# FNet and mixture-of-experts kernel: half of six blocks' residuals by an adding DMA, a check moved among the experts, two rows' statistics on VectorE

## Chip, core and metric

One core of a Trainium2 chip. The metric is the device time of one execution in microseconds (us). The engines that matter are TensorE (PE, matmuls; PEld is its weight load), VectorE (DVE), ScalarE (ACT), GpSimd (POOL), and SyncE (SP), which issues most DMAs. Each engine runs its own queue in order and waits at semaphores for the others.

## What is computed

Two layers on 2048 tokens of width 512, cut to the core:

```python
x = A_x
# FNet: Fourier transform over hidden and sequence, real part
n = layernorm(x)
a = einsum("bsd,ed->bse", n, dft_hid_re)
b = einsum("bsd,ed->bse", n, dft_hid_im)
h = x + einsum("ts,bse->bte", dft_seq_re, a) - einsum("ts,bse->bte", dft_seq_im, b)
# mixture of 8 experts, each token to its best one (gate: softmax of one value)
f = layernorm(h)
e = argmax(f @ w_gate)
h2 = h + gate * (silu(f @ w1[e]) @ w2[e])
```

## The kernel before

**First stage (0 to some 235 us): the FNet.** The sequence-side transform comes first. The 2048 rows of `x` arrive in four groups ("quads") `xq[0..3]` of 512 rows, that is four row tiles q of 128 rows each. For each group VectorE and ScalarE compute the layer norm's statistics (`far_stats` on ScalarE for the row tiles in `SIDE`, `own_stats` on VectorE for the others), fold the rows (`turned`, `mirror`, `mix`) and round them into `xh[g]` (`spread`) and into `fold[g]` (`high` for the high part `fh`, `low_part` for the low part `fl`).

The matrix of the sequence transform arrives in 32 blocks n, each for a 256-column chunk c and a group g (`PLAN`): blocks 0 to 7 are chunks 0 and 1 of groups 0 to 3 in turn, two blocks per group, while the later blocks belong to one chunk after another. A block is two loads of 512 KB, `raw` i = 0 and i = 1 (`load_w`, four buffers in a ring). `high_w(n)` has ScalarE copy 256 + 256 + 256 columns of the first half into `hold` (rounded to fp32r, the third part negated). `rest_w(n)` has VectorE form the residual of each half, `raw` minus or plus a window of `hold`, into `pair` (line 367): four row tiles of 512 columns, q = 0, 1 from i = 0 and q = 2, 3 from i = 1. TensorE multiplies: `residual` (line 720) takes `pair` against `xh[g]`, `folded` (line 731) takes `hold` against `fold[g]`, `outer` (line 735) two edge rows. The first four groups are one Python loop over g; blocks 2g and 2g + 1 are used in group g. When chunk 0 is summed (after block 6), `evacuate` copies its sums from PSUM (ScalarE lines 686 to 700, VectorE 692). From block 8 on (`step`) the loop is over chunks; in the first of these steps also the hidden-side matrices `dh`, `ds`, `dd` are prepared (`prep_d`, lines 408 to 422), and `second` (line 644) multiplies the evacuated chunk by them, token tile by token tile, beside the next chunks.

**A check.** The roundings only hold if the residuals are small. `gauge(n)` queues, for every block, ScalarE's sum of squares of the residuals q = 1 to 3 (`square`, line 371), one for each block into `rsum`, and for g = 0 that of `hold` into `hsum`; `settle` puts queued squares into the order a few blocks later. After the FNet, `order()` (in steps among the first expert's) compares them, and `ctl` says whether a slow repair at the end must run.

**Second stage (to some 545 us): the experts.** Eight experts r, 11 steps j each. In a step, `prep` makes the next step's weights: ScalarE rounds a 512 KB load (`far`, in the first expert `raw`) into the high half of `pair` (line 131) and VectorE subtracts the low half (line 132); `first` does 12 matmuls `hp` from them, ScalarE the Silu, VectorE `hh` and `hl`; `then` does the second product two steps later. GpSimd gathers and scatters token rows by indirect DMAs; `o` and `yT` are VectorE's and ScalarE's outgoing tiles.

**What sets the order.** On TensorE, VectorE, ScalarE and SP the order is that of the Python code (`manual_schedule`). GpSimd's is set by the scheduler of the language. A DMA that waits for a semaphore holds up what is queued behind it on its issuing engine.

Of the kernel before, what the change touches and what calls it, by code (L numbers as in the profile page):

```python
# [8 lines left out]
F32 = mybir.dt.float32  # L9
F32R = mybir.dt.float32r  # L10
# [3 lines left out]
ALU = mybir.AluOpType  # L14
# [11 lines left out]
NC = S // TC  # L26
NJ = (F + P - 1) // P

DEFER = 4
HOT = (1, 0, 2, 3)  # L30
EARLY, LATE = 240, 64
# [26 lines left out]
def fnet_moe(ctx: ExitStack, tc: tile.TileContext, xquad, xedge, xres, wseq, wedge, dhid, dmix, wcol, wexp, out):  # L58
# [44 lines left out]
    peek = const.tile([NL, 8], F32, name="peek")  # L103
    nc.vector.tensor_scalar(base, start_at, float(EARLY - P), 1.0, op0=ALU.is_lt, op1=ALU.add)
    rsum = const.tile([P, NT], F32, name="rsum")
    hsum = const.tile([P, NC], F32, name="hsum")
    rsumd = const.tile([P, KD], F32, name="rsumd")
    hsumd = const.tile([P, KD // 2], F32, name="hsumd")
# [84 lines left out]
    with ExitStack() as pa:  # L193
# [7 lines left out]
        def ap(t, at, dims):  # L201
            return bass.AP(tensor=t.tensor, offset=t.offset + at, ap=[list(t.ap[0])] + dims)
# [139 lines left out]
        def load_w(n, some=range(2)):  # L342
            if n < NT:
                c, g = PLAN[n]
                for i in some:
                    t = wraw[n, i] = ring.tile([P, 2 * D], F32, name="raw", bufs=RAWS)
                    nc.sync.dma_start(t, wseq[c, g, i])

        def high_w(n):
            settle(n - 4)  # L350
            if n < NT:
                a = wraw[n, 0]
                h = his[n] = hbuf[:, n % QN, :]
                nc.scalar.copy(h[:, :2 * TC], a[:, :2 * TC])
                nc.scalar.mul(h[:, 2 * TC:], a[:, :TC], -1.0)  # L355

        def rest_w(n, some=range(2)):

            if n >= NT:
                return  # L360
            if n not in res:
                res[n] = ring.tile([P, QN, D], F32R, name="pair", bufs=4)
            window = ap(his[n].bitcast(F32), 0, [[TC, 2], [1, 2 * TC]])
            odd = ORDER[PLAN[n][0]][0]
            for i in some:
                w = wraw.pop((n, i)).rearrange("p (q c) -> p q c", q=2)
                nc.vector.tensor_tensor(res[n][:, 2 * i:2 * i + 2, :], w, window, op=ALU.add if odd and i else ALU.subtract)  # L367

        def square(out, src, n):
            junk = work.tile([P, 3 * D], BF16, name="junk", bufs=1)  # L370
# [3 lines left out]

        def gauge(n):

            c, g = PLAN[n]
            at = c * QN + g
            r, h = res[n][:, 1:, :].rearrange("p q c -> p (q c)"), his[n][:, TC:2 * TC]
            pending.append((n, lambda: square(rsum[:, at:at + 1], r.bitcast(F32), 3 * D)))  # L380
            if g == 0:
                pending.append((n, lambda: square(hsum[:, c:c + 1], h.bitcast(F32), TC)))
# [3 lines left out]
                pending.pop(0)[1]()  # L386
                most -= 1

        dh, ds, dd = [[keep.tile([P, 2, D], F32R, name=f"{n}{i}") for i in range(KD // 2)] for n in ("dh", "ds", "dd")]
        wk = keep.tile([P, KD, E], F32, name="wk")  # L390
        draw = {}

# [368 lines left out]

        def prep_w(n):
            rest_w(n)
            load_w(n + 2)

        xes, first_e = prep_xe(), prep_e(0)

# [32 lines left out]
        spread(0, CB, r2)  # L800
        rest_w(0, (1,))
        load_w(2)

        for g in range(QN):
# [341 lines left out]
    with ExitStack() as pb:  # L1146
# [169 lines left out]
        def order():  # L1316
# [40 lines left out]
            nbs = work.tile([P, 1], F32, name="nbs")  # L1357
            nc.vector.reduce_sum(nbs, nb, axis=AX.X)
            nc.vector.tensor_copy(nbi, nbs)
            yield  # L1360
            good = work.tile([P, NT + KD], F32, name="good")
            most = work.tile([P, NC], F32, name="most")
            nc.vector.tensor_scalar(most, hsum, SMALL, None, op0=ALU.mult)
# [16 lines left out]
            nc.vector.tensor_scalar(ctl[:, 2:3], fine, float(NC), None, op0=ALU.mult)  # L1380
            nc.vector.tensor_add(fine, fine, nbs)
            nc.vector.tensor_scalar(ctl[:, 0:1], fine, 0.0, None, op0=ALU.is_gt)

        def look_up(r):

# [9 lines left out]
        ordering = order()  # L1395

        for n in range(len(steps) + LAG):
            if n < len(steps):
# [2 lines left out]
                    prep(NA + n + 1)  # L1401
                if r == 0 and j:
                    next(ordering, None)
                if r + 1 < E:

                    if j == (3 if r == 0 else 0):
                        look_up(r + 1)
                        wheres[r + 1] = whence(tab[r + 1][0])
                    if j == (4 if r == 0 else 1):
                        xgs[r + 1] = gather("xg", frows, wheres[r + 1][0], pieces(CAPS[r + 1]))  # L1410
                    if j == 8:
                        src, ids = wheres.pop(r + 1)
                        hgs[r + 1] = gather("hg", hrows, src, pieces(CAPS[r + 1])), ids, tab[r + 1][1]
# [10 lines left out]
            if n >= LAG:  # L1424
# [14 lines left out]
                    going = back(hgs.pop(q), yT, pieces(CAPS[q]))  # L1439
                if j < NQ and r:  # L1440
                    next(going, None)
        q, yT = done.pop()
        for _ in back(hgs.pop(q), yT, pieces(CAPS[q])):
            pass
# [279 lines left out]
```

## Time and profile before

| | |
|---|---|
| median of 3 runs | 557.08 us (556.95 to 558.57) |
| the profiled execution | 556.46 us, span of the trace 554.7 us |
| busy, TensorE | 523.7 us, 94% |
| busy, VectorE | 421.0 us, 76% |
| busy, ScalarE | 313.2 us, 56% |
| mean granted TensorE clock | 0.966 |
| HBM read | 99.63 MB |

Shares of the whole span mix two stages with different limits, so a table of busy times by stretch comes first, then who waited for whom in a stretch, then the single instructions of an engine in order of time. A row of the timeline is: start, duration, engine, line and operation, out<-in, form, count, and in brackets the idle time before it and who ended it.

### The profile page before, as it was taken

How to read it: one execution, taken by the hardware profiler on the slowest of the kernel's cores; microseconds unless marked ns; L12 is line 12 of the kernel's file. 1: busy time of each engine (PE TensorE's matmuls, PEld its weight loads, DVE VectorE, ACT ScalarE, POOL GpSimd, SP SyncE). 2: the span in 40 equal slices, each digit the busy share in tenths (PEclk: the TensorE clock that was granted, in tenths of full speed). 3: DMA queues.
4: the chain of work that ended last, by engine and by line, in shares of the span. 5: the costliest groups of instructions: out<-in, count | busy, mean ns of one | idle time of the engine just before them, and what ended most of it. 6: DMA issues, size and time to landing. Idle time of an engine off the chain costs nothing. (4 is left out here: it accounts for less than half of the span.)

```text
span 554.7 us, 9722 instructions
## 1 busy us (share of the span) xinstructions
PE 523.7 (94%) x3478; PEld 477.1 (86%) x3478; DVE 421.0 (76%) x916; ACT 313.2 (56%) x566; POOL 80.2 (14%) x112
## 2 busy tenths in 40 slices
PE   6886979999999999999999999999999999999992
PEld 2665768999998999998999999999999999999991
DVE  6999999997886678767686766867778777777751
ACT  5799985659582555465544444445455555555540
POOL 2000000000000000001250620431503223130201
PEclk9586998999999999999999999999999999999997
DMA  8767647565767666545185664765757667585401
GB/s 309 250 229 254 209 166 259 188 208 193 253 225 238 209 210 223 182 157 195 48 308 229 224 207 146 229 198 194 220 196 228 230 228 264 182 275 186 151 1 43
DMA packets 36458, 112.95 MB, mean 204 GB/s; under 512 B 4670, under 2 KB 4670, under 8 KB 36400
## 3 DMA queue, kind: packets, MB, share of 16 engines
q1 hardware_dynamic: 32144, 99.38, 54.2%
q0 software_dynamic: 4256, 12.85, 6.7%
q8 instruction: 30, 0.49, 0.4%
q14 instruction: 28, 0.23, 0.1%
HBM read 99.63 MB, written 12.78 MB: 203 GB/s over the span
## 5 line engine op out<-in xcount | busy, mean ns | idle before, releaser
L132 DVE TENSOR_TENSOR pair<-far,pair 128x1024 fp32r<-128x1024 f32 x77 | 94.3, 1225 | 55.2 <-ACT pair L131 55.2
L131 ACT CAST pair<-far 128x1024 fp32r<-128x1024 f32 x77 | 80.9, 1050 | 75.7 <-PE yp L167 75.7
L720 PE MATMUL p<-pair,xh 128*128 128x512 f32 (+1 forms) x480 | 104.0, 344 | 16.9 <-DVE pair L367 12.9
L720 PEld LDWEIGHTS p<-pair,xh 128*128 128x128 f32 x480 | 78.2, 203 | 30.0 <-DVE pair L367 12.7
L165 PE MATMUL hp<-th,pair 128*128 128x256 f32 (+3 forms) x308 | 88.3, 287 | 0.0
L166 PE MATMUL hp<-tl,pair 128*128 128x256 f32 (+3 forms) x308 | 87.4, 284 | 0.0
L167 PE MATMUL hp<-th,pair 128*128 128x256 f32 (+3 forms) x308 | 87.3, 283 | 0.0
L367 DVE TENSOR_TENSOR pair<-raw,hold 128x1024 fp32r<-128x1024 f32 x64 | 75.7, 1217 | 7.0 <-ACT hold L355 4.1
L1211 ACT ACTIVATE sl<-hp 128x256 f32<-128x256 f32 (+4 forms) x88 | 34.7, 395 | 48.5 <-PE hp L167 48.5
L731 PE MATMUL p<-hold,fh 128*128 128x256 f32 x240 | 59.6, 288 | 0.0
L165 PEld LDWEIGHTS hp<-th,pair 128*128 128x128 f32 x308 | 58.0, 188 | 1.9
L166 PEld LDWEIGHTS hp<-tl,pair 128*128 128x128 f32 x308 | 57.9, 188 | 1.6
L167 PEld LDWEIGHTS hp<-th,pair 128*128 128x128 f32 x308 | 57.9, 188 | 0.0
L165 PE MATMUL yp<-hh,pair 128*128 128x304 f32 (+3 forms) x176 | 52.8, 300 | 0.0
L166 PE MATMUL yp<-hl,pair 128*128 128x304 f32 (+3 forms) x176 | 51.2, 291 | 0.0
L167 PE MATMUL yp<-hh,pair 128*128 128x304 f32 (+3 forms) x176 | 51.2, 291 | 0.0
L371 ACT ACTIVATE junk<-pair 128x1536 bf16<-128x1536 f32 x32 | 47.3, 1479 | 0.0
L731 PEld LDWEIGHTS p<-hold,fh 128*128 128x128 f32 x240 | 45.1, 198 | 1.1
L731 PE MATMUL p<-hold,fl 128*128 128x256 f32 x152 | 42.8, 291 | 0.0
L1259 POOL DMA_INDIRECT out_h<-o,ids x20 | 30.4, 1520 | 79.9 <-DVE o L1258 79.1
L1215 DVE TENSOR_TENSOR hl<-sl,hh 128x256 fp32r<-128x256 f32 (+4 forms) x88 | 38.5, 438 | 3.0
L165 PE MATMUL yp<-pair,hl 128*128 128x512 f32 x88 | 35.8, 407 | 0.0
(322 smaller groups left out, 1078.5 us busy)
## 6 DMA issues: line engine op xcount, KB each, us to landing
far<-in_wexp SPq DMA_DIRECT2D x77, 512.0 KB, 3.7
raw<-in_wseq SPq DMA_DIRECT2D x64, 512.0 KB, 4.7
raw<-in_wexp SPq DMA_DIRECT2D x11, 512.0 KB, 4.4
big<-in_xquad SPq DMA_DIRECT2D x8, 512.0 KB, 5.8
xt<-in_xres SPq DMA_DIRECT2D x16, 256.0 KB, 5.3
hrows<-row SPq DMA_DIRECT2D x16, 256.0 KB, 4.5
frows<-row SPq DMA_DIRECT2D x13, 256.0 KB, 4.6
big<-in_dmix SPq DMA_DIRECT2D x3, 512.0 KB, 6.6
```

The lines of the kernel that those rows point to most:

```text
L131: nc.scalar.copy(hi, src)
L132: (eng or nc.vector).tensor_sub(lo, src, hi.bitcast(F32))
L165: nc.tensor.matmul(ps, sl, mh, start=first, stop=False)
L166: nc.tensor.matmul(ps, sh, ml, start=False, stop=False)
L167: nc.tensor.matmul(ps, sh, mh, start=False, stop=last)
L367: nc.vector.tensor_tensor(res[n][:, 2 * i:2 * i + 2, :], w, window, op=ALU.add if odd and i else ALU.subtract)
L371: nc.scalar.activation(junk[:, :n], src, AF.Square, accum_out=out)
L720: nc.tensor.matmul(out, xh[g][:, q, k * P:(k + 1) * P], mv, start=first, stop=False)
L731: nc.tensor.matmul(out, s, mv, start=False, stop=False)
L1211: nc.scalar.activation(sl, ps, AF.Silu)
L1215: nc.vector.tensor_sub(hl, sl, hh.bitcast(F32))
L1259: d = nc.gpsimd.indirect_dma_start(out=out, out_offset=bass.IndirectOffsetOnAxis(ap=ids[:n, i:i + 1], axis=0), in_=o[:n], in_offset=None, ...
```

## The change

1. For the six blocks 2 to 7 (`ADDS`), the residual of the second half (q = 2, 3) is no longer formed by VectorE from a loaded `raw`. GpSimd issues a DMA that copies the window of `hold` into the block's place, and behind it a DMA that adds the block's second half from DRAM onto it (`accum_op`). In these blocks `load_w` loads only the first half, which lets loads be issued earlier (`LOADS`). Blocks 2, 3 and 4 get places of their own, `homes`, a tile in which later `dh`, `ds` and `dd` lie.
2. `high_w` of the odd blocks moves: block 3 to the end of the first group's preparation, block 5 and 7 likewise, one group earlier than before.
3. `gauge` does nothing for blocks 0 to 7. In its place `recheck` loads both halves of each of these blocks again (16 loads of 512 KB) among the experts from the second on, in `raw` buffers; ScalarE copies and negates, VectorE forms both residuals (128x512 and 128x1024), ScalarE squares them; one piece in each step, six steps for a block. The comparison and `ctl` follow it.
4. `SIDE[2]` is empty: all four rows' statistics of group 3 are VectorE's.

```diff
+ADDS = range(2, 8)
+LOADS = {1: (4, 5), 2: (6,), 3: (7,), 4: (8,), 5: (), 6: (9,), 7: ()}
+ANEW = 8
...
                 for i in some:
+                    if i and n in ADDS:
+                        continue
                     t = wraw[n, i] = ring.tile([P, 2 * D], F32, name="raw", bufs=RAWS)
                     nc.sync.dma_start(t, wseq[c, g, i])
...
                 h = his[n] = hbuf[:, n % QN, :]
                 nc.scalar.copy(h[:, :2 * TC], a[:, :2 * TC])
                 nc.scalar.mul(h[:, 2 * TC:], a[:, :TC], -1.0)
+                if n in ADDS:
+                    c, g = PLAN[n]
+                    nc.gpsimd.dma_start(home(n)[:, 2:4, :], windows(n))
+                    nc.gpsimd.dma_start(home(n)[:, 2:4, :], wseq[c, g, 1].rearrange("p (q c) -> p q c", q=2), accum_op=ALU.add)
...
             for i in some:
+                if i and n in ADDS:
+                    continue
                 w = wraw.pop((n, i)).rearrange("p (q c) -> p q c", q=2)
...
         def gauge(n):
 
+            if n < ANEW:
+                return
...
-        SIDE = (CB,(3,),CB)
+        SIDE = (CB,(3,),())
...
-            high_w(2 * g + 1)
+            if not g:
+                high_w(1)
...
                 settle(2 * g - 1)
+                high_w(2 * g + 3)
                 upper(g + 1, r2)
...
+        def recheck():
+
+            for n in range(ANEW):
+                c, g = PLAN[n]
+                at = c * QN + g
+                a, b = [ring.tile([P, 2 * D], F32, name="raw", bufs=RAWS) for _ in range(2)]
+                for i, t in enumerate((a, b)):
+                    nc.sync.dma_start(t, wseq[c, g, i])
+                yield
+                yield
+                h = ring.tile([P, 2 * D], F32, name="raw", bufs=RAWS)
+                nc.scalar.copy(h[:, :D].bitcast(F32R), a[:, :D])
+                nc.scalar.mul(h[:, D:D + TC].bitcast(F32R), a[:, :TC], -1.0)
+                yield
+                nc.vector.tensor_sub(a[:, D:], a[:, D:], h[:, TC:TC + D])
+                yield
+                window = bass.AP(tensor=h.tensor, offset=h.offset, ap=[list(h.ap[0]), [TC, 2], [1, D]])
+                b2 = b.rearrange("p (q c) -> p q c", q=2)
+                nc.vector.tensor_tensor(b2, b2, window, op=ALU.add if ORDER[c][0] else ALU.subtract)
+                nc.scalar.activation(a[:, D:], a[:, D:], AF.Square, accum_out=rsum[:, at:at + 1])
+                yield
+                if g == 0:
+                    nc.scalar.activation(h[:, TC:2 * TC], h[:, TC:2 * TC], AF.Square, accum_out=hsum[:, c:c + 1])
+                nc.scalar.activation(b, b, AF.Square, accum_out=rsum1[:, at:at + 1])
+                yield
...
+                if r > 0:
+                    next(checking, None)
```

GpSimd's queue, from its last small constants to the first DMA of the second half of the FNet. Before, nothing stands there:

```order
L125 MEMSET xlow_105 2x1 x3
L125 MEMSET wlow_106 4x1 x3
L1009 DMA peek_99<-frows_144 13x8
L1012 MEMSET hold_2825 128x1
L1085 TENSOR_SCALAR src0_2911<-table_96 128x2
```

With the change (L370 is the copy of a `hold` window, L371 the adding DMA; `homes_169` holds blocks 2, 3 and 4, `pair_481` block 5, `pair_590` block 6, `pair_631` block 7):

```order
L129 MEMSET wlow_106 4x1 x3
L370 DMA homes_169<-hold_168 128x2x512 x2
L371 DMA homes_169<-in_wseq 128x1024 x2
L370 DMA homes_169<-hold_168 128x2x512
L370 DMA pair_481<-hold_168 128x2x512
L371 DMA homes_169<-in_wseq 128x1024
L371 DMA pair_481<-in_wseq 128x1024
L370 DMA pair_590<-hold_168 128x2x512
L371 DMA pair_590<-in_wseq 128x1024
L370 DMA pair_631<-hold_168 128x2x512
L371 DMA pair_631<-in_wseq 128x1024
L1035 DMA peek_99<-frows_145 13x8
```

In the first two groups both copies stand ahead of both sums; blocks 6 and 7 have copy and sum each by itself.

ScalarE's queue in the third group (g = 2), from the rounding of the edge rows (`xe`, L454) to the norm's `qn`. Before (L226 and L227 are the statistics of two rows, L295 is `fh`, L354 and L355 `hold` of blocks 5 and 6, L371 a square of the check):

```order
L454 CAST xe_175<-qn_211 96x512
L354 CAST hold<-raw 128x512
L355 ACTIVATE hold<-raw 128x256
L226 ACTIVATE junk,nm_596<-big 128x512
L227 ACTIVATE junk,mv_595<-big,nm_596 128x512
...
L295 CAST fh_610<-row 128x1024
L371 ACTIVATE junk,rsum<-pair 128x1536
L354 CAST hold<-raw 128x512
L355 ACTIVATE hold<-raw 128x256
L249 ACTIVATE sd_626<-mv_595,eps 128x4
L459 ACTIVATE xe_176<-xe_175,own_group 96x512
```

With the change (the same operations at other lines; `hold` is now that of blocks 6 and 7):

```order
L476 CAST xe_171<-qn_207 96x512
L299 CAST fh_585<-row 128x1024
L366 CAST hold<-raw 128x512
L367 ACTIVATE hold<-raw 128x256
L253 ACTIVATE sd_607<-mv_582,eps 128x4
L481 ACTIVATE xe_172<-xe_171,own_group 96x512
L481 ACTIVATE xe_173<-xe_171,own_group 96x512
L481 ACTIVATE xe_171<-xe_171,own_group 96x512
L366 CAST hold<-raw 128x512
L367 ACTIVATE hold<-raw 128x256
L293 ACTIVATE qn_207<-big,r_612 128x512 x2
```

The statistics and the square are gone, block 6's `hold` stands right behind `fh`, and block 7's behind the three `xe`, ahead of `qn`.

## Rows read from the trace of the kernel before

**Rows 1.** Busy time of each engine by stretch: stretch in us, its length, then busy us (and instructions) of PE, PEld, DVE, ACT, POOL, the granted TensorE clock as a share of full speed, the busy share of the 16 DMA engines, GB/s.

```profile
28.00:42.00 14.00, 10.88 (x60) 8.97 (x58) 13.00 (x36) 12.91 (x28) 0.00 (x0) 0.88 0.68 226
42.00:56.00 14.00, 9.95 (x39) 8.37 (x40) 13.79 (x31) 13.79 (x28) 0.00 (x0) 0.63 0.74 261
56.00:70.00 14.00, 12.90 (x85) 11.08 (x84) 12.94 (x20) 13.94 (x26) 0.00 (x0) 1.00 0.65 217
70.00:84.00 14.00, 10.44 (x66) 9.10 (x66) 13.42 (x15) 12.27 (x24) 0.00 (x0) 0.97 0.46 163
84.00:98.00 14.00, 14.00 (x75) 12.44 (x74) 13.76 (x22) 6.76 (x13) 0.00 (x0) 0.91 0.73 239
350.00:400.00 50.00, 50.00 (x402) 49.10 (x401) 35.59 (x63) 23.62 (x37) 17.95 (x13) 1.00 0.68 212
```

**Rows 2.** Who TensorE waited for: the first two rows from 14 to 84 us, the third from 84 to 545 us, each with us in total, times, the longest.

```profile
PE p L720 <- DVE pair L367: 12.9, 9, 3.2
PE p L720 <- ACT xh L283: 0.8, 1, 0.8
...
PE hp L165 <- ACT sl L1211: 0.2, 1, 0.2
```

**Rows 3.** VectorE's timeline: residuals (L367), the statistics of a row (L236).

```profile
26.21 2.35 DVE L367 TENSOR_TENSOR pair<-raw,hold 128x1024 fp32r<-128x1024 f32 x2
...
32.04 2.36 DVE L367 TENSOR_TENSOR pair<-raw,hold 128x1024 fp32r<-128x1024 f32 x2 [0.83 <-ACT hold L355]
...
48.73 2.35 DVE L367 TENSOR_TENSOR pair<-raw,hold 128x1024 fp32r<-128x1024 f32 x2
51.00 0.68 DVE L236 BATCH_NORM_STATS2 st<-big 128x6 f32<-128x512 f32 x1
...
51.81 0.66 DVE L236 BATCH_NORM_STATS2 st<-big 128x6 f32<-128x512 f32 x1
...
63.25 4.62 DVE L367 TENSOR_TENSOR pair<-raw,hold 128x1024 fp32r<-128x1024 f32 x4
...
70.21 2.36 DVE L367 TENSOR_TENSOR pair<-raw,hold 128x1024 fp32r<-128x1024 f32 x2 [0.69 <-ACT hold L355]
...
80.64 3.49 DVE L367 TENSOR_TENSOR pair<-raw,hold 128x1024 fp32r<-128x1024 f32 x3
```

**Rows 4.** ScalarE's timeline: a square of the check (L371), `hold` (L354, L355), `fh` (L295), `sd` (L249), the three `xe` (L459).

```profile
34.31 1.48 ACT L371 ACTIVATE junk<-pair 128x1536 bf16<-128x1536 f32 x1
...
46.30 0.62 ACT L354 CAST hold<-raw 128x512 fp32r<-128x512 f32 x1
46.82 0.41 ACT L355 ACTIVATE hold<-raw 128x256 fp32r<-128x256 f32 x1
...
50.20 1.03 ACT L295 CAST fh<-row 128x1024 fp32r<-128x1024 f32 x1
...
53.59 0.30 ACT L249 ACTIVATE sd<-mv,eps 128x4 f32<-128x4 f32 x1
53.79 2.07 ACT L459 ACTIVATE xe<-xe,own_group 96x512 fp32r<-96x512 f32 x3
```

**Rows 5.** TensorE's timeline: residual products (L720) and folded ones (L731), and the first hidden-side product (L644). Block 5 begins at 50.00, block 6 at 59.22, block 7 at 65.61, block 8 at 70.42, block 10 at 81.91.

```profile
50.00 3.21 PE L720 MATMUL p<-pair,xh 128*128 128x512 f32 x8 [1.77 <-DVE pair L367]
...
55.56 0.41 PE L731 MATMUL p<-hold,fh 128*128 128x256 f32 x1
...
59.22 3.77 PE L720 MATMUL p<-pair,xh 128*128 128x512 f32 x16 [0.76 <-ACT xh L283]
...
65.61 1.54 PE L720 MATMUL p<-pair,xh 128*128 128x512 f32 x8
...
70.42 1.07 PE L720 MATMUL p<-pair,xh 128*128 128x512 f32 x4
...
78.47 0.28 PE L731 MATMUL p<-hold,fh 128*128 128x256 f32 x1
81.91 0.73 PE L720 MATMUL p<-pair,xh 128*128 128x512 f32 x2 [3.16 <-DVE pair L367]
83.04 1.17 PE L720 MATMUL p<-pair,xh 128*128 128x512 f32 x2 [0.40 <-DVE pair L367]
84.01 0.41 PE L731 MATMUL p<-hold,fh 128*128 128x256 f32 x1
...
86.36 0.71 PE L644 MATMUL y<-dh,big 128*128 128x512 f32 x2
```

**Rows 6.** DMAs: first the 512 KB loads of `raw` from 14 to 84 us, us from issue to landing; then GpSimd's gathers of 256 KB at L1170, duration of the issue in ns and us to landing; and the page's row of the queue that SP's DMAs run on (packets, MB, share of 16 engines over the span).

```profile
DMA to landing us min/median/max: 3.2/4.7/5.9
...
L1170 POOL DMA_INDIRECT hg<-hrows,src x17: 895/1182/1897, 283.2 to 494.3; - x17
...
DMA to landing us min/median/max: 3.3/5.1/7.2
...
q1 hardware_dynamic: 32144, 99.38, 54.2%
```

**Rows 7.** Experts: VectorE's making of the next weights' low part (L132) in two steps that follow each other, and TensorE's first matmul with the second one's result.

```profile
453.11 1.23 DVE L132 TENSOR_TENSOR pair<-far,pair 128x1024 fp32r<-128x1024 f32 x1 [0.92 <-ACT pair L131]
...
455.91 1.29 DVE L132 TENSOR_TENSOR pair<-far,pair 128x1024 fp32r<-128x1024 f32 x1 [0.25 <-ACT pair L131]
...
457.44 0.28 PE L165 MATMUL hp<-th,pair 128*128 128x256 f32 x1
```

More of the change, by code (lines that the diff above doesn't have):

```diff
@@ L105, in fnet_moe @@
     rsum = const.tile([P, NT], F32, name="rsum")
+    rsum1 = const.tile([P, ANEW], F32, name="rsum1")
     hsum = const.tile([P, NC], F32, name="hsum")
@@ L345, in load_w, with home @@
                 for i in some:
+                    if i and n in ADDS:
+                        continue
                     t = wraw[n, i] = ring.tile([P, 2 * D], F32, name="raw", bufs=RAWS)
                     nc.sync.dma_start(t, wseq[c, g, i])
+        def home(n):
+            if n not in res:
+                j = n - ADDS.start
+                res[n] = homes[:, QN * j:QN * j + QN, :] if 0 <= j < 3 else ring.tile([P, QN, D], F32R, name="pair", bufs=4)
+            return res[n]
         def high_w(n):
@@ L355, in high_w, with windows @@
                 nc.scalar.mul(h[:, 2 * TC:], a[:, :TC], -1.0)
+                if n in ADDS:
+                    c, g = PLAN[n]
+                    nc.gpsimd.dma_start(home(n)[:, 2:4, :], windows(n))
+                    nc.gpsimd.dma_start(home(n)[:, 2:4, :], wseq[c, g, 1].rearrange("p (q c) -> p q c", q=2), accum_op=ALU.add)
+        def windows(n):
+            return ap(his[n], 0, [[TC, 2], [1, 2 * TC]])
         def rest_w(n, some=range(2)):
@@ L360, in rest_w @@
                 return
-            if n not in res:
-                res[n] = ring.tile([P, QN, D], F32R, name="pair", bufs=4)
-            window = ap(his[n].bitcast(F32), 0, [[TC, 2], [1, 2 * TC]])
+            out, window = home(n), windows(n).bitcast(F32)
             odd = ORDER[PLAN[n][0]][0]
             for i in some:
+                if i and n in ADDS:
+                    continue
                 w = wraw.pop((n, i)).rearrange("p (q c) -> p q c", q=2)
-                nc.vector.tensor_tensor(res[n][:, 2 * i:2 * i + 2, :], w, window, op=ALU.add if odd and i else ALU.subtract)
+                nc.vector.tensor_tensor(out[:, 2 * i:2 * i + 2, :], w, window, op=ALU.add if odd and i else ALU.subtract)
         def square(out, src, n):
@@ L387, in settle @@
                 most -= 1
-        dh, ds, dd = [[keep.tile([P, 2, D], F32R, name=f"{n}{i}") for i in range(KD // 2)] for n in ("dh", "ds", "dd")]
+        homes = keep.tile([P, 3 * QN, D], F32R, name="homes")
+        dh, ds, dd = [[homes[:, 2 * (KD // 2 * j + i):2 * (KD // 2 * j + i) + 2, :] for i in range(KD // 2)] for j in range(3)]
         wk = keep.tile([P, KD, E], F32, name="wk")
@@ L763, in prep_w @@
             rest_w(n)
-            load_w(n + 2)
+            for m in LOADS.get(n, (n + 2,)):
+                load_w(m)
         xes, first_e = prep_xe(), prep_e(0)
@@ L802, in fnet_moe @@
         load_w(2)
+        load_w(3)
         for g in range(QN):
@@ L1359, in order @@
             nc.vector.tensor_copy(nbi, nbs)
+            told.append(nbs)
+        def recheck():
[22 more added lines that the diff above has]
+                yield
+            nc.vector.tensor_add(rsum[:, :ANEW], rsum[:, :ANEW], rsum1)
             yield
+            nbs, = told
             good = work.tile([P, NT + KD], F32, name="good")
@@ L1382, in order @@
             nc.vector.tensor_scalar(ctl[:, 0:1], fine, 0.0, None, op0=ALU.is_gt)
+            yield
         def look_up(r):
@@ L1393, in look_up @@
             tab[r] = (u[:, :, 0], u[:, :, 1])
-        ordering = order()
+        told = []
+        ordering, checking = order(), recheck()
         for n in range(len(steps) + LAG):
@@ L1441, in fnet_moe @@
                     next(going, None)
+        for _ in checking:
+            pass
         q, yT = done.pop()
```

## Prediction

> **What bounds the kernel now.** I read the windows first. From 84 us on TensorE has no gap (14.00 of 14.00, later 50.00 of 50.00), while from 28 to 84 us it is busy 10 to 13 of 14 and VectorE 12.9 to 13.8 [rows 1]. The table of waits names the pair: all that TensorE waits for between 14 and 84 us is 12.9 us for `pair<-L367` (VectorE's residuals) and 0.8 for ScalarE; after 84 us it is 0.2 [rows 2]. So in the first 84 us VectorE's queue is the bound, and afterwards TensorE, so that each us by which TensorE gets earlier to the row at 86.36 (the first hidden-side matmuls) is one us of the span, and what is added later costs only where it makes TensorE wait. ScalarE is nearly full too between 42 and 70 us (13.8, 13.9). One more thing is to be seen: after a wait of 1.77 us a 256-column matmul takes 0.41 us instead of 0.28 from 50.00 until 55.6, and the granted clock of that stretch is 0.63; after the wait of 3.16 us at 81.91 it is 0.41 again [rows 1, 5]. A long wait thus costs its length and then a stretch at 1.2 GHz; a wait of 0.76 us (59.22) cost no such thing.
>
> **What leaves VectorE.** Of six blocks (2 to 7) one of the two residuals goes: two take 2.35 us and four 4.62, so each further one 1.14, 6.8 in all. Block 3 also loses its wait of 0.83 for ScalarE's `hold`, since `high_w(3)` now runs where ScalarE idled [rows 3]. Two rows' statistics come back in the third group: from 51.00 to 51.81 is one row, so 1.6 for two. VectorE's lead over before is then: 1.1 after block 2, 3.1 after block 3, 4.2 after block 4, 5.4 after block 5, 3.8 after the statistics, 6.1 after blocks 6 and 7. The work behind them (63.25 to 80.64) leaves VectorE little idle time, 0.6 of 14 us from 70 to 84, which is the wait at 70.21 [rows 1, 3], so block 10's residual, at 80.64, comes at about 74.5 and its two halves at 75.7 and 76.9. If no one else were late, that is the gain.
>
> **What leaves ScalarE.** Eight squares of 1.48 us, and two rows' statistics, from the end of the row at 46.82 to 50.20, 3.0 us [rows 4]. ScalarE was not what TensorE waited for, so I count nothing for it alone; it only lets the two `hold` instructions, on which the new copies wait, be early.
>
> **What is added on the DMA queues, the price that no row has.** Each of the six blocks now needs a copy (SBUF to SBUF, 512 KB) and behind it an adding DMA (512 KB from DRAM), both issued by GpSimd, the second after the first has landed; TensorE's third matmul of the block waits for the second. Let S be the time from the end of `hold` to the landing of the sum. For the copy: a load of the same size takes 4.7 us from issue to landing in this stretch (3.2 to 5.9), and GpSimd's own issue is longer than SP's, 0.9 to 1.9 us with a median of 1.2, for which I add 0.3: 5.0 [rows 6]. The sum reads its target as well: one more passage of 512 KB, which at the queue's own rate (99.38 MB in 54.2% of 554.7 us, 331 GB/s) is 1.6 us, so 6.6. S is 11.6, an estimate. Its low end is two of the quickest landings and the second passage, 3.2 + 3.2 + 1.6 = 8.0; its high end the slowest landing of a GpSimd transfer, 7.2 us for half the bytes, enlarged by 1.6 for the other half, and again with the second passage: 8.8 + 10.4 = 19.2. I take the value near the load, since size, place and traffic are the same.
>
> The Trainium skill, "DMA: Bandwidth & Descriptors", section "Anatomy of one DMA", gives about 2.0 us and bytes over 436 GB/s for a GpSimd transfer: 3.2 us here, and S would be 6.4 (an estimate from that page, and without the second passage). The loads of [rows 6] are at 4.7, so the trace doesn't bear it out while queues are busy.
>
> **Which sums are late.** GpSimd's queue is in the order of two copies, two sums, two copies, two sums, then copy and sum of block 6 and of block 7, so a sum waits for the next block's `hold` in the first two groups. There TensorE has room, 3.1 and 4.0 idle us in two windows [rows 1]: it will wait at the third matmul of blocks 2 and 4, which by itself moves nothing, since VectorE and ScalarE don't wait for TensorE until block 6 is through. Block 4's `hold` ends near 34.3, where the first square began [rows 4] (`hold` of block 3 has left the place ahead of it, its own has come), its sum lands at 45.9, and the 10 us of matmuls of that window end by 56 to 58. It is with blocks 6 and 7 that the sums count. Block 6's `hold` follows `fh` at once: 46.30 less 3.1 of lead, 1.0 for `fh`, 0.9 for `hold`: 45.1. Its sum lands at 56.7, when its `xh` is ready as well (59.22 less 3.8 is 55.4, all four parts a little later), and about when TensorE has block 5 behind it. Block 7's `hold` stands behind `sd` and the three `xe`: `sd` comes when the statistics end, 53.59 less 5.4 and plus 1.6 is 49.8 at most and about 48.9 since it no longer waits for the small instructions ahead of it; then 0.2, 2.07 and 0.9: 52.1 [rows 4]. Its sum lands at 52.1 + S = **63.7**.
>
> TensorE needs 6.4 us at most for block 6 (59.22 to 65.61), and less now since its `xh` are all there, so from 61 or 62 on it waits for 63.7. Block 7 takes 4.8 us before (65.61 to 70.42), 0.4 of it done ahead of the wait. With a wait of over 1.7 us the next 5.6 to 5.8 us run at 1.2 GHz, as after 50.00: 5.8 us do 2.9 of those 4.4, the other 1.5 run at full speed: 7.3. Blocks 8 and 9 take 8.3 (70.42 to the end of 78.47's row). Then block 10, already there (76.9): before, the work between 81.91 and 86.36 took 4.05 us without the 0.40 wait, at 1.2 GHz, so 2.0 now [rows 5]. 63.7 + 7.3 + 8.3 + 2.0 = 81.3 against 86.36: **5.0 us** earlier. The rule behind it: the gain is 16.6 - S, until VectorE binds.
>
> **What is added among the experts.** Eight blocks' check: 16 loads of 512 KB, and on VectorE 8 instructions of 1.2 and 8 of half that, on ScalarE five or six short ones for each block. By busy time it is covered: 36 of 50 us on VectorE, 24 on ScalarE, DMA 0.68 [rows 1]. What counts is the single step, in which VectorE makes the next weights' low part just ahead of TensorE. In the step at 453.11 VectorE idles 0.25 us in front of the next one at 455.91, which ends at 457.20, and TensorE takes the result at 457.44 [rows 7]. A check of 1.14 there makes it late by 0.9, and TensorE waits 0.6. Of the sixteen pieces three fall in such steps (beside an `o`, a `yT` or a `look_up`); the rest fall into steps with more room (from 350 to 400 us 14.4 us are idle over some 17 steps, 0.8 each), where a long one is late by 0.3, which the 0.24 between 457.20 and 457.44 nearly takes up. Two long pieces at 0.6 and a short one at about 0.1 make 1.3 us. The bounds are 0 and 5.2 (all eight long ones at 0.65).
>
> **The sum.** 5.0 less 1.3 is 3.7. The profiled execution took 556.46 us (span 554.7) and would take 552.8; the median of the runs is 0.6 above it, so 557.1 - 3.7 = **553.4**.
>
> **The rivals.** (A) The sums land quickly: with S at 8.0 block 7's is there at 60.1, TensorE doesn't stop, block 7 ends near 65.7, blocks 8 and 9 at 74.0, and VectorE's block 10 (second half 76.9, then 1.6 of full-speed work) binds: 78.5, 7.9 earlier, 6.6 net: 550.5. For it speaks that the traffic of SP is thinner here than before; against it that no load of this size was under 3.2. The page's 3.2 us for a transfer would give this same result. (B) The sums land late and the change is slower: with S at 19.2 the gain is 16.6 - 19.2 = -2.6, and with the experts' 1.3 the time is 561.0. It turns from S = 15.3, where net gain ends. For it: the landing of 7.2 us for half the bytes, an adding DMA that may not stream as a copy does, and 12 further transfers on engines that are 0.65 to 0.74 busy. (C) The checks cost as much as the front gains: at 4 to 5.2 us the time is 556.1 to 557.3, no change. For it: steps of 2.8 us with a quarter us of idle time (453.11 to 455.91); against it, the 0.8 in the mean step. (D) GpSimd's issue, and not the transfer, sets S: at 1.9 us for each of the two issues, the longest seen, in place of 1.2, S grows by 1.4, the gain is 3.6, and the time 554.8. VectorE's instructions with two inputs, which fill this stretch, would have to stand in GpSimd's way. The Trainium skill, "SBUF — State Buffer", section "Who interferes with whom", has such a lock for VectorE's copies and against GpSimd's reads, not for two-input instructions against what GpSimd writes; no run so far shows which.
>
> **How the numbers follow.** Forecast and D together 0.45 (551.5 to 555.5), A 0.17, C 0.16, B 0.22. A measurement tells about 0.3%, 1.7 us. Faster by that are A and nearly all of forecast and D: 0.61. Within it are C and the edge of forecast and D: 0.17. Slower is B, 0.22. The range is 549.8 (A with half of the checks' cost) to 559.5 (B up to S near 17.7); above lies about a tenth.
>
> **What will show it.** The issues of the sums, with their time to landing (6.6), the copies (5.0); TensorE's wait for the sum of block 7 at about 61 to 64 us, and none for block 10; the first hidden-side matmul near 81; granted clock low around 64 to 69. Among the experts a few waits of TensorE under 1 us, on `pair`, in three steps. The prediction is wrong if a sum takes over 9 us, if TensorE waits at block 10 still, or if the experts' steps from the second expert on get longer by more than 2 us in all.

## The result, and the profile after

The changed kernel takes 561.54 us (median of 8 runs, 559.58 to 563.25) against 557.12 (8 runs, 556.47 to 558.57): a ratio of 1.0078 with a 95% interval of 1.0064 to 1.0091. It is slower by 0.8%, where 553.4 was forecast. One of the seven runs of E3 below was slow (647.5 us, mean granted clock 0.744): it counts in E3's median, not in its ratio. The profiled execution has a span of 559.7 us; before, 554.7. Lines have moved: residual products L720 to L742, the first hidden-side product L644 to L666, VectorE's residuals L367 to L386, the experts' weight split L132 to L136; the copy is L370, the sum L371.

First the windows of the changed kernel, columns as in [rows 1]:

```profile
28.00:42.00 14.00, 8.47 (x46) 7.51 (x47) 13.73 (x40) 12.01 (x26) 2.37 (x4) 0.76 1.01 275
42.00:56.00 14.00, 8.38 (x43) 7.36 (x42) 13.62 (x32) 9.21 (x17) 2.55 (x3) 0.76 0.96 257
56.00:70.00 14.00, 9.12 (x66) 8.03 (x64) 6.66 (x10) 5.82 (x13) 2.46 (x3) 1.00 1.01 349
70.00:84.00 14.00, 9.32 (x49) 8.63 (x50) 13.58 (x17) 9.00 (x18) 0.00 (x0) 0.76 0.47 121
84.00:98.00 14.00, 14.00 (x95) 12.83 (x94) 11.85 (x19) 7.18 (x15) 0.00 (x0) 1.00 0.78 255
```

Up to 70 us the 16 DMA engines are now full (0.96 to 1.01, before 0.65 to 0.74 [rows 1]), and TensorE is less busy in every window up to 84. VectorE, full before, has 6.66 of 14 us between 56 and 70: it is no longer the bound there. TensorE's waits from 14 to 110 us (us in total, times, longest) say who is:

```profile
PE p L742 <- DMA homes<-in_wseq: 10.9, 2, 5.6
PE p L742 <- DMA pair<-in_wseq: 9.6, 2, 6.0
PE p L742 <- DVE pair L386: 2.9, 3, 2.2
```

Before, VectorE's residuals held TensorE up for 12.9 us [rows 2]. Now it is 2.9, and 20.5 us go to the sums. GpSimd's timeline (start, length, idle time before and what ended it) has the last six of its twelve issues:

```profile
43.98 0.92 POOL L371 DMA_DIRECT2D homes<-in_wseq  x1 [6.78 <-DMA homes<-hold]
45.11 0.89 POOL L371 DMA_DIRECT2D pair<-in_wseq  x1 [0.21 <-issue]
45.77 0.97 POOL L370 DMA_DIRECT2D pair<-hold  x1
58.06 0.87 POOL L371 DMA_DIRECT2D pair<-in_wseq  x1 [11.32 <-DMA pair<-hold]
59.11 0.73 POOL L370 DMA_DIRECT2D pair<-hold  x1 [0.18 <-ACT hold L367]
67.41 0.86 POOL L371 DMA_DIRECT2D pair<-in_wseq  x1 [7.57 <-DMA pair<-hold]
```

The first two are the sums of blocks 4 and 5. Block 6's copy is issued at 45.77, its sum 12.3 us later, when the copy has landed. Block 7's copy stands behind that sum in the queue: ScalarE ended its `hold` at 52.6 (row below), the copy is issued at 59.11. ScalarE's two rows of the `hold` of blocks 6 and 7, and TensorE's rows of block 6, block 7 and the first hidden-side product:

```profile
45.00 0.41 ACT L367 ACTIVATE hold<-raw 128x256 fp32r<-128x256 f32 x1
...
52.15 0.41 ACT L367 ACTIVATE hold<-raw 128x256 fp32r<-128x256 f32 x1
```

```profile
63.62 2.13 PE L742 MATMUL p<-pair,xh 128*128 128x512 f32 x14 [3.55 <-DMA pair<-in_wseq]
...
74.68 2.08 PE L742 MATMUL p<-pair,xh 128*128 128x512 f32 x6 [6.01 <-DMA pair<-in_wseq]
...
91.38 3.82 PE L666 MATMUL y<-homes,big 128*128 128x512 f32 x16
```

S, the time from the end of `hold` to the landing of the sum (taken as TensorE's start behind its wait), is 63.6 - 45.4 = 18.2 us for block 6 and 74.7 - 52.6 = 22.1 for block 7; the forecast had 11.6. The hidden side starts at 91.38 instead of 86.36 [rows 5], 5.0 us late, as much as the span has grown. How long the transfers took, copies first, then sums (least, median, most), and the page's rows of the queues (packets, MB, share of 16 engines over the span):

```profile
DMA to landing us min/median/max: 3.5/8.1/11.9
...
DMA to landing us min/median/max: 5.4/7.3/9.2
```

```profile
q1 hardware_dynamic: 33584, 104.63, 55.3%
q0 software_dynamic: 6752, 19.14, 11.4%
```

Here q0 is GpSimd's queue and q1 SP's. From 46 to 50 us, with block 6's copy just issued, their shares are

```profile
q0 software_dynamic: 174, 0.65, 91.7%
q1 hardware_dynamic: 19, 0.08, 5.9%
```

So what the copy first stands behind is not SP's traffic but GpSimd's own two sums, those of blocks 4 and 5. SP's next three loads, issued from 46.66 on, share the engines after that: from 50 to 54 us the shares are 56.5% and 47.8%.

VectorE kept the lead that was forecast, and then lost it by waiting for block 6's evacuation:

```profile
53.52 1.22 DVE L386 TENSOR_TENSOR pair<-raw,hold 128x1024 fp32r<-128x1024 f32 x1
...
58.45 3.49 DVE L386 TENSOR_TENSOR pair<-raw,hold 128x1024 fp32r<-128x1024 f32 x3
69.02 0.69 DVE L714 TENSOR_TENSOR big<-p,big 128x512 fp32r<-128x512 f32 x1 [7.08 <-ACT big L722]
```

Among the experts the first and the last split of a weight from `far` on VectorE start at 305.49 and 543.62 us, 238.1 apart; before, at 301.21 and 536.38, 235.2 apart. So the checks cost 3.0 us there. TensorE's waits after 300 us show 1.9 of them:

```profile
PE tp L1431 <- DVE fineb L1428: 1.1, 1, 1.1
PE hp L169 <- DVE pair L136: 0.8, 2, 0.4
```

The account of the span: 4.3 us late at the first of these splits, 3.0 more at the last, and 2.2 less from there to the end (16.1 against 18.3 us): +5.0.

### The profile page after: what moved, and what is told of

Same layout as the page of the kernel before. It is cut to its first block, busy times and chain, and to the rows that moved or that the text cites. A ratio compares the mean times of both kernels' runs of the same rounds, so it can differ in the third digit from the quotient of the medians.

```text
span 559.7 us, 9803 instructions
## 1 busy us (share of the span) xinstructions
PE 518.9 (93%) x3476; PEld 474.2 (85%) x3478; DVE 429.5 (77%) x930; ACT 316.6 (57%) x590; POOL 93.2 (17%) x124
## 3 DMA queue, kind: packets, MB, share of 16 engines
q1 hardware_dynamic: 33584, 104.63, 55.3%
q0 software_dynamic: 6752, 19.14, 11.4%
## 5 line engine op out<-in xcount | busy, mean ns | idle before, releaser
L136 DVE TENSOR_TENSOR pair<-far,pair 128x1024 fp32r<-128x1024 f32 x77 | 94.2, 1224 | 44.7 <-ACT pair L135 44.6
L742 PE MATMUL p<-pair,xh 128*128 128x256 f32 (+1 forms) x440 | 92.6, 337 | 15.6 <-DMA pair<-in_wseq 9.6
L742 PEld LDWEIGHTS p<-pair,xh 128*128 128x128 f32 x440 | 70.9, 199 | 24.7 <-DMA pair<-in_wseq 6.4
L386 DVE TENSOR_TENSOR pair<-raw,hold 128x1024 fp32r<-128x1024 f32 x55 | 65.2, 1217 | 4.7 <-ACT hold L367 2.8
L753 PE MATMUL p<-hold,fh 128*128 128x256 f32 x240 | 57.4, 281 | 0.0
L666 PE MATMUL p<-homes,big 128*128 128x512 f32 x208 | 50.5, 395 | 0.0
L666 PEld LDWEIGHTS p<-homes,big 128*128 128x128 f32 x208 | 38.1, 188 | 7.5
L753 PEld LDWEIGHTS p<-hold,fh 128*128 128x128 f32 x240 | 43.2, 190 | 1.1
L753 PE MATMUL p<-hold,fl 128*128 128x256 f32 x152 | 40.9, 281 | 0.0
```

The costliest lines, as they stand in the source:

```text
L136: (eng or nc.vector).tensor_sub(lo, src, hi.bitcast(F32))
L386: nc.vector.tensor_tensor(out[:, 2 * i:2 * i + 2, :], w, window, op=ALU.add if odd and i else ALU.subtract)
L666: nc.tensor.matmul(ps, st, mv, start=n == 0, stop=n == 8 * KD // 2 - 1)
L742: nc.tensor.matmul(out, xh[g][:, q, k * P:(k + 1) * P], mv, start=first, stop=False)
L753: nc.tensor.matmul(out, s, mv, start=False, stop=False)
```

## The experiments

Theories: **T1**, the DMA engines have more work than they can do up to 70 us, so every transfer takes longer; **T2**, the transfers stand in line and GpSimd's queue holds block 7's copy back; **T3**, the adding, and not the transfer as such, is what costs; **T4**, the checks among the experts. All runs of a group stand beside runs of the kernel before (556.7 to 557.4 us).

**E1. No sums by DMA.**

```diff
-ADDS = range(2, 8)
-LOADS = {1: (4, 5), 2: (6,), 3: (7,), 4: (8,), 5: (), 6: (9,), 7: ()}
+ADDS = range(2, 2)
+LOADS = {}
...
-        load_w(3)
```

> The changed kernel with no sums by DMA: VectorE forms both halves of all blocks again and the loads come in the order of before; the checks among the experts and the two rows' statistics on VectorE stay. If the loss is the late sums of blocks 6 and 7 (first hidden-side matmul at 91.4 us after, 86.4 before), that matmul goes back to 86 to 88 us (two rows' statistics more on VectorE) and the time to 557.5 to 560.0 us, what is left over 557.1 being the checks. If the loss is made by the checks among the experts and the late front is hidden by them, the time stays within 1 us of 561.5.

558.03 us, ratio 1.0014 (0.9998 to 1.003). The hidden side starts at 85.56 us, a little ahead of the expected 86 to 88. The loss in the front is that of the copies and sums (the loads go back to the order of before with them). Its experts, 238.15 us between the same two splits, are as long as after the change, with no sums at all: the 3.0 us belong to the checks. On the page of this kernel the queue of GpSimd has

```profile
q0 software_dynamic: 4256, 12.85, 6.5%
```

so that copies and sums together are 11.4% of 559.7 less 6.5% of 556.8: 27.6 us of all 16 engines, in the first 75. (The shares are rounded to 0.1%, some 0.5 us here, and what else runs on this queue is taken as equal in both.)

**E2. The squares where they were, no checks among the experts.**

```diff
-ANEW = 8
+ANEW = 0
...
```

> The changed kernel with the squares of the first eight blocks where they were before and no second loading among the experts; the sums by DMA stay. If the checks among the experts cost what the last scatter shows (7.2 us late, of which the first weight split of the experts is 4.3 late already), the time falls by 1.5 to 3 us, to 558.5 to 560.0. If they are hidden, it stays at 561.5 within 0.7. If squares that wait for a sum stop ScalarE's evacuation in the first 100 us, it is over 562.

563.34 us, ratio 1.0115 (1.0074 to 1.0155). The time is the third case's: the hidden side starts at 93.47, 2.1 us later than in the changed kernel, and the experts take 235.7 us, 2.4 less. The way there is another than was expected. ScalarE, with 11.1 us more work between 14 and 98 us, makes `hold`, on which the copies wait, later (block 6's ends at 48.8 instead of 45.4, and its sum is issued at 59.24 instead of 58.06), while its evacuation still waits for TensorE and not for squares. Moving the checks away did serve the sums.

**E3. ScalarE writes the window, only the sum is a DMA.**

```diff
-                    nc.gpsimd.dma_start(home(n)[:, 2:4, :], windows(n))
+                    nc.scalar.copy(home(n)[:, 2:4, :], windows(n).bitcast(F32))
```

> The changed kernel with the window written into its half by ScalarE instead of by a copying DMA; only the summing DMA stays on GpSimd's queue. If the loss is the two transfers in line and GpSimd's queue between them, a sum takes 1 us (ScalarE) and 5.4 to 9.2 us (landing of the sums after) from its hold: block 6's is in by 54 to 56 us and block 7's by 60 to 63, before VectorE's last halves, so that TensorE waits for VectorE or for nothing there, and the first hidden-side matmul comes at 81 to 84 us: 551 to 555 us. If summing in flight is what is slow, and grows to 15 us or more as the copies did, the time is 557 or more.

553.98 us, ratio 0.9944 (0.9923 to 0.9965), within the first theory's range. From 14 to 110 us TensorE waits for no DMA any more. The sums of blocks 6 and 7 in GpSimd's timeline, the queue, and the first hidden-side product:

```profile
46.80 0.86 POOL L371 DMA_DIRECT2D pair<-in_wseq  x1 [7.47 <-ACT pair L370]
54.02 0.85 POOL L371 DMA_DIRECT2D pair<-in_wseq  x1 [6.35 <-ACT pair L370]
```

```profile
q0 software_dynamic: 5120, 16.00, 9.8%
```

```profile
80.59 3.96 PE L666 MATMUL y<-homes,big 128*128 128x512 f32 x16 [0.48 <-DVE big L714]
```

Block 7's sum is issued 13.4 us sooner than in the changed kernel. The queue gives prices: six sums are 9.8% of 550.6 less 36.2, that is 17.8 us of the 16 engines, 3.0 each; the six copies are the other 9.8 us, 1.6 each. A load on SP's queue is 1.55 (55.3% of 559.7 us for 104.63 MB, 512 KB of it).

**E4. Another order on GpSimd's queue, by the order of the code.**

```diff
-                    nc.gpsimd.dma_start(home(n)[:, 2:4, :], wseq[c, g, 1]..., accum_op=ALU.add)
+                    for m in {6: (), 7: (6, 7)}.get(n, (n,)):
+                        c, g = PLAN[m]
+                        nc.gpsimd.dma_start(home(m)[:, 2:4, :], wseq[c, g, 1]..., accum_op=ALU.add)
```

> The changed kernel with one change of order on GpSimd's queue: the copy of block 7 stands ahead of the sum of block 6. If the wait in the queue is the loss (copy of block 7 ready at 52.6 us, issued at 59.1), the copy lands 6.5 us sooner, the sum of block 7 by 68 to 70 us instead of 74.7, and the time is 556 to 558.5 us. If the DMA engines are full there (busy share 0.96 to 1.01 between 28 and 70 us), both transfers only share them, the sum of block 7 is in at 72 us or later, and the time is 559.5 to 561.5.

561.47 us, ratio 1.0091 (1.0059 to 1.0123), but it tells nothing: the scheduler, which orders GpSimd's queue by itself, put block 7's copy behind block 6's sum again (58.16, then 59.20 us).

**E5. The same order, by an edge.**

```diff
+                    copied = nc.gpsimd.dma_start(home(n)[:, 2:4, :], windows(n))
+                    for m in {6: (), 7: (6, 7)}.get(n, (n,)):
+                        with tc.issue_after(copied.ins):
...
```

> The changed kernel with GpSimd's queue in another order, now by an edge between the instructions: copy of block 6, copy of block 7, sum of block 6, sum of block 7. If the wait in the queue is the loss, the copy of block 7 is issued at 52.7 us instead of 59.1, the sum of block 7 is in at 68 to 70 us instead of 74.7, the first hidden-side matmul comes at 85 to 87 us instead of 91.4 and the time is 556 to 558.5 us. If full DMA engines are the loss (busy share 0.94 to 1.05 from 14 to 70 us), the two copies and the sums share them, the sum of block 7 is in at 72 us or later and the time is 559.5 to 561.5.

560.42 us, ratio 1.0049 (1.0032 to 1.0066); the profile is of its slowest run, 562.42. GpSimd's last three issues, then block 6 and the hidden side on TensorE, and the window from 66 to 70 us:

```profile
52.96 0.75 POOL L370 DMA_DIRECT2D pair<-hold  x1 [6.48 <-ACT hold L367]
58.09 0.92 POOL L374 DMA_DIRECT2D pair<-in_wseq  x1 [4.39 <-DMA pair<-hold]
61.82 0.88 POOL L374 DMA_DIRECT2D pair<-in_wseq  x1 [2.81 <-DMA pair<-hold]
```

```profile
64.90 3.75 PE L745 MATMUL p<-pair,xh 128*128 128x512 f32 x14 [5.30 <-DMA pair<-in_wseq]
...
90.72 4.06 PE L669 MATMUL y<-homes,big 128*128 128x512 f32 x16
```

```profile
66.00:70.00 4.00, 4.00 (x20) 3.90 (x19) 0.00 (x0) 0.00 (x0) 0.00 (x0) 0.50 1.05 263
```

Both theories had a part of it. The copy goes out 6.2 us sooner, its sum 5.6 sooner, and TensorE has no wait for block 7 any more, as T2 wanted. But block 6, which now shares the engines with that copy, comes 1.3 us later (64.90 for 63.62), TensorE had waited 5.30 us and runs at half clock (0.50) until 70, so that block 6's 14 products take 3.75 us instead of 2.13; the evacuation behind block 6 is late, and VectorE behind that. The hidden side gains 0.7 us in this profile and the time falls where T1 had it. The queue's wait was real and, put right by itself, worth 1.1 us by the medians and 1.6 by the ratios, of the 7.5 that E3 gained.

**E6. Plain loads in place of the sums.** The load writes over the window that was copied there, so this kernel leaves the window out of these residuals.

```diff
-..., wseq[c, g, 1].rearrange("p (q c) -> p q c", q=2), accum_op=ALU.add)
+..., wseq[c, g, 1].rearrange("p (q c) -> p q c", q=2))
```

> The changed kernel with the summing DMAs replaced by plain loads of the same 512 KB to the same place: the sums of blocks 2 to 7's second halves are left out. From the queue's shares a copy takes the 16 engines 1.64 us, a sum 2.96 and a load on SP's queue 1.55. If the sums' double work on full engines is the loss, six plain loads save some 8.5 us of engine time up to 70 us, block 7's half is in by 69 to 72 us and the time is 556 to 559 us. If two transfers in line and the queue between them are the loss whatever they do, the time stays within 1 us of 561.5.

553.99 us, ratio 0.9946 (0.9926 to 0.9966), faster than either expectation. GpSimd's last four issues, the queue, and TensorE:

```profile
45.63 0.71 POOL L370 DMA_DIRECT2D pair<-hold  x1 [3.65 <-ACT hold L367]
51.18 0.56 POOL L371 DMA_DIRECT2D pair<-in_wseq  x1 [4.84 <-DMA pair<-hold]
52.76 0.70 POOL L370 DMA_DIRECT2D pair<-hold  x1 [1.03 <-ACT hold L367]
58.77 0.55 POOL L371 DMA_DIRECT2D pair<-in_wseq  x1 [5.30 <-DMA pair<-hold]
```

```profile
q0 software_dynamic: 6752, 19.14, 10.3%
```

```profile
57.40 3.52 PE L742 MATMUL p<-pair,xh 128*128 128x512 f32 x14 [1.15 <-DMA pair<-in_wseq]
...
81.46 3.96 PE L666 MATMUL y<-homes,big 128*128 128x512 f32 x16 [0.49 <-DVE big L714]
```

The two transfers are still in line, in the same queue and order. The copy of block 6 takes 5.6 us from issue to the next issue instead of 12.3, the copy of block 7 finds the queue free, and block 6's S is 57.4 - 45.4 (its `hold` ended as before) = 12.0. The same packets and bytes take 1.1% of the span less, 7.1 us of the 16 engines, 1.2 for each transfer: a sum costs the engines 3.0 us where a plain load by the same queue costs 1.8. So the adding fills the engines (T3 by way of T1), and it is the next copies that pay: the loads of blocks 4 and 5 are issued at 40.22 and 41.43 here, 4.2 us and more ahead of block 6's copy, where the sums had 43.98 and 45.11.

**E9. Other loads out of the way.** In the changed kernel, the three loads of the hidden-side matrices (`in_dmix`, the "decay matrices" of the expectation) behind the next blocks' loads.

```diff
-            elif g + 2 == QN:
-                for k in (0, 2, 1):
-                    load_d(k)
-            else:
-                load_d(3)
+            elif g + 2 > QN:
+                for k in (0, 2, 1, 3):
+                    load_d(k)
```

> The changed kernel with the three 512 KB loads of the decay matrices, which stood on SP's queue at 46.7 to 48.2 us, moved behind the loads of the next blocks, to some 60 us; sums and copies stay. If full DMA engines are the loss, the copy of block 6 loses 4.6 us of the engines' work ahead of and beside it (three loads of 1.55 us), lands by 54 us instead of 57.7, block 7's sum is in by 71 to 73 us instead of 74.7, unless the moved loads meet it there, and the time is 558.5 to 560.5 us. If the loads on SP's queue don't matter to GpSimd's transfers, 561.5 within 0.7.

561.05 us, ratio 1.0066 (1.0043 to 1.0088): in time no more than the second theory has. The transfers show both sides. GpSimd's last four issues:

```profile
45.58 0.73 POOL L370 DMA_DIRECT2D pair<-hold  x1 [0.28 <-issue]
54.61 0.87 POOL L371 DMA_DIRECT2D pair<-in_wseq  x1 [8.30 <-DVE pair L386]
55.66 0.73 POOL L370 DMA_DIRECT2D pair<-hold  x1 [0.18 <-ACT xh L287]
65.00 0.86 POOL L371 DMA_DIRECT2D pair<-in_wseq  x1 [8.61 <-DMA pair<-hold]
```

Without the three loads beside it block 6's copy has its sum behind it after 9.0 us instead of 12.3 (T1). The 9.0 that are left are still far from 5.6 in E6: GpSimd's queue, with the two sums, has 93.0% of the engines from 46 to 50 us. Whether the copy waits for these sums in line on its queue or for its share of the engines, no run tells apart. Then the moved loads meet block 7's transfers: copy to sum 9.3 instead of 8.3, and TensorE gets the sum at 74.40 for 74.68. Here work on full engines was put off, not saved.

**E7 and E8. The checks.** E7 is E3 with one more `yield` between the count `fineb` and its matmul; E8 is E3 without the check's loop.

```diff
             yield
+            yield
             ct = pt.tile([P, D], F32, name="tp")
             nc.tensor.matmul(ct[:, :1], ones, fineb, start=True, stop=True)
```

> The kernel with ScalarE's window (554.0 us) and one step more between the count of the good rows on VectorE and the matmul that adds it up, in the experts. TensorE waited 1.1 us there, with all else in its queue behind it. If that wait is on the path, 552.9 us (552.4 to 553.4); if the wait is taken up later, 554.0 within 0.4.

> The kernel with ScalarE's window (554.0 us) without the check of the first eight blocks among the experts: their 16 loads, casts, differences and squares are left out, the count at the end stays. If the checks cost what lies between the experts' first and last weight split (238.1 us with them, 235.2 before: 2.9 us, 1.1 of it at the count's matmul, which stays), the time falls by 1.5 to 2 us, to 552.0 to 552.5; if they are hidden but for that matmul, it stays at 553.5 to 554.5.

E7 takes 552.78 us, ratio 0.9916 (0.99 to 0.9933); E8 552.60, ratio 0.9916 (0.9894 to 0.9938). In E7 the wait of 1.1 us is gone and the time falls by 1.2. In E8 that wait stays, the waits on `pair` are gone, and the splits lie 236.4 us apart instead of 238.1. So of the checks' 3.0 us (T4) 1.1 is the wait at the count's matmul and 1.7 the loop's own work; E8's 0.1 above its range's end is within the scatter.

**E10 and E11. Which line is late in the new front.** E10 is E7 with one of the two rows' statistics back on ScalarE; E11 also puts the cast of block 6 ahead of that row.

```diff
-SIDE = (CB,(3,),())
+SIDE = (CB,(3,),(3,))
...
+            if g == 2:
+                high_w(2 * g + 2)
             if more:
                 got = far_stats(xq[g + 1], range(QN), SIDE[g])
...
-            high_w(2 * g + 2)
+            if g != 2:
+                high_w(2 * g + 2)
```

(all but `SIDE` only in E11)

> The kernel with ScalarE's window and the later matmul (552.8 us), and of the two rows' statistics that the change moved to VectorE one back on ScalarE. In the trace of that kernel VectorE has the statistics of four rows from 45.93 to 49.13 us and ScalarE waits 3.0 us for them. A row costs VectorE 0.85 us and ScalarE 1.64. If VectorE's line sets the front's end, each step behind is 0.85 us earlier and the time is 551.7 to 552.3 us; if TensorE's waits come from elsewhere, 552.8 within 0.4.

> The kernel with one row's statistics back on ScalarE (554.4 us), and in the third group the cast of block 6 to its hold, with the window, put ahead of that row's statistics on ScalarE. There the statistics had pushed hold and window back by 1.6 us (45.20 to 46.76), the sum of block 6 was issued at 48.1 instead of 46.7 and TensorE waited 1.75 us until 58.39. If that sum undid VectorE's gain of 0.6 us, the sum is issued by 46.6 us, block 6 runs by 57 us and the time is 551.7 to 552.6 us. If it was something else (a lower granted clock by chance, ScalarE's line), the time stays at 553.5 to 555.

E10 takes 554.40 us (551.59 to 555.60), ratio 0.995 (0.993 to 0.997): slower than E7, as neither expectation had it. E11 takes 552.37, ratio 0.991 (0.989 to 0.993). Block 6's sum in GpSimd's timeline, E10 and then E11:

```profile
48.10 0.85 POOL L371 DMA_DIRECT2D pair<-in_wseq  x1 [8.94 <-ACT pair L370]
```

```profile
45.81 0.86 POOL L371 DMA_DIRECT2D pair<-in_wseq  x1 [6.54 <-ACT pair L370]
```

In E10 the row's statistics push `hold` back, the sum goes out 1.6 us later than in E7 (46.54) and lands 10.2 us after that, block 6 goes on at 58.39 and the granted clock from 56 to 70 us is 0.76 (0.88 in E7). With the sum out at 45.81 all of it is back. VectorE's line alone would have given 0.85 us; E11's 0.4 below E7 is less than these runs can tell. So what moved E10 and E11 was the start of block 6's sum, not VectorE's statistics; with one profile of each this rests on E11 having come out as its first theory said.

**E12. E1 with E7's `yield`.**

> The kernel with no sums by DMA (558.0 us), with the later matmul in the experts. If the 1.1 us wait is on the path here too, 556.9 us (556.4 to 557.4), that is, within 0.1% of before, and the sums with ScalarE's window are worth the rest, 4 us, to 552.8; if it is taken up later, 558.0 within 0.5.

557.27 us, ratio 0.9993 (0.9981 to 1.0006), no wait at the count left. Beside E7 this is the worth of the sums when the window costs no transfer: 0.77% or some 4.3 us. Of the kernels that leave nothing out, E3, E7, E10 and E11 beat both kernels.

## Why the prediction was wrong

**Right: what bounded the kernel, and VectorE's part.** VectorE's last residuals of that stretch end at 61.9 instead of 67.9 [rows 3], 5.9 us of lead where 6.1 was said; `hold` of blocks 6 and 7 end at 45.4 and 52.6 (45.1 and 52.1 said). Counting nothing for ScalarE was too little: with the squares left on it (E2) it would have made the holds late.

**Wrong: the term S**, "copy 5.0, sum 6.6", 11.6 us; it was 18.2 and 22.1. The sum was nearly right (7.3 at the median), the copy was not (3.5 to 11.9, median 8.1), and block 7's copy stood 6.5 us behind block 6's sum in GpSimd's queue. The 22.1 are 6.5 of this wait, 8.3 from the copy's issue to the sum's, and 7.3 for the sum. By the prediction's numbers the wait was nothing (45.1 + 5.0 is 50.1, ahead of block 7's `hold` at 52.1): it comes from block 6's copy, which took 12.3 us to its sum. The price of the copy was taken from loads on engines that were 0.7 busy, while the change itself fills them: copies and sums are 27.6 us of the 16 engines (E1, E3), the six loads that go 9.3, so 18.3 more, nearly all of it in the 56 us from 14 to 70, of which some 17 were free (a busy share of 0.72 to 28 us, then 0.65 to 0.74 [rows 1]). The rows at hand would have shown most of this: twelve transfers at 1.6 us, and the sums' second passage, are 28.8. E6 shows that the term was the error: with plain loads block 6's S is 12.0, TensorE doesn't wait for block 7's half, the hidden side starts at 81.46 (81.3 said) and the time is 554.0 (553.4 said). That these agree so closely is in part luck: in E6 TensorE waits for VectorE at block 10 (1.40 us), which the prediction ruled out, and smaller errors in the experts and at the end make up for each other. E5 shows that the queue's wait alone is worth 1 to 2 us.

**Right, but for its clock: the rule that follows from S**, "the gain is 16.6 - S": with 22.1 it is -5.5, and the hidden side is 5.0 late. Its term for the clock was misread, at little cost: the low clock did not begin with the wait of 1.77 us at 50.00, it was 0.50 from 46 to 50 us already, and the 0.63 for 42 to 56 us [rows 1] says so too: 5.6 us at half speed would leave 0.80. Nor did every long wait bring it: behind the 3.55 us ahead of block 6 in the changed kernel the clock stayed at 1.00. Block 7, behind a wait of 6.01 us, took 6.4 us (74.68 to 81.06) where 7.3 was said.

**Too small: the checks among the experts**, 1.3 said, 3.0 measured. The steps with little room were found (0.8 us of waits on `pair`), the matmul of the count, which now sits in a busy step and stops TensorE for 1.1 us, was not.

**The rivals.** B, late sums, decided it, for two of the reasons written there (a sum doesn't stream as a copy does, twelve further transfers); that its 561.0 is so near 561.5 is luck, with S at 19.2 and smaller checks, the shorter end making up for both. A is out, no sum took under 5.4. C was 3.0, too little to matter by itself. D is out: GpSimd's issues took 0.7 to 1.0 us, less than the 1.2 taken.

**Open** stays the end. From the last weight split to the end of the span it is 15.6 to 16.5 us in the kernels that have twelve transfers more on GpSimd's queue (after, E2, E4, E5, E6, E9) and 17.6 to 18.5 in those with six or none (before, E1, E3, E7, E8, E10 to E12). The instructions of that stretch are the same. The difference lies behind the issue of the last scatter, which ends at 545.7 us before and 552.9 after, 9.0 and 6.8 us ahead of the end, when no compute engine works any more; no run was made for it. Some 2 us of the change's loss are given back there.

## What to carry to other kernels

Before work is moved to the DMA engines, add up what it takes of all 16 of them in that stretch, beside what is there; a landing time read while they have room no longer holds when they are full. Of two transfers in line, replace the one that an engine with room can do (the window on ScalarE, 1.05 us an instruction, was worth 7.5 us), and look at what stands behind a waiting issue in GpSimd's queue. A check that is moved to a quiet place still has a last step that stops somebody: give its result a step of room before TensorE takes it.

## What the hardware showed that I had not expected

An adding DMA of 512 KB from DRAM took the 16 engines 3.0 us, a plain one by the same queue 1.8, a copy within SBUF 1.6, a load by SP's queue 1.55 (E1, E3 and E6, from the queues' shares). The traffic of GpSimd slowed that of SP: the decay matrices' loads took 10.6 us to land instead of 6.6. The Trainium skill, "DMA: Bandwidth & Descriptors", section "Issuing engines are not separate DMA queues", says that DMAs of all issuing engines run on the same 16 engines and interleave; the trace agrees, with these numbers, a share of 1.01, and 56.5% for GpSimd's queue beside 47.8% for SP's from 50 to 54 us. From 46 to 50 us, with two sums under way, the engines were 0.98 busy and moved 181 GB/s by the profile's count, against 412 GB/s from 42 to 44 us: a full engine need not be a fast one. In E5 a wait of 5.30 us on TensorE was followed by four us at half the clock (0.50), so that there a late transfer cost more than its lateness; behind 3.55 us in the changed kernel it did not.
